# Filler matmuls in the waits of the layer ends, the last V tiles used in parts, and the last K transposed ahead of other VectorE work

## The chip, the cores and the metric

The kernel runs on one core of a Trainium2 chip. The metric is the time of one execution on the device, in microseconds (us). A profile's span runs from the first to the last instruction; in the runs here the time is 1.8 to 2.8 us longer than the span, mostly 1.9. The engines are called PE (TensorE), DVE (VectorE), ACT (ScalarE), POOL (GpSimd) and SP (SyncE, which issues the transfers). Lines such as L492 are lines of the kernel that was profiled.

## The reference, cut to what matters

Two layers, each a decode step of attention over a long cache, then a gated MLP. Batch 4, one query position, 32 query heads on 8 groups of K and V, 4096 cached positions, head size 128, all in bfloat16. Both layers read the same caches and weights.

```python
def _A_ref(x, k_cache, v_cache, wq, wo):        # caches: 4 x 8 x 4096 x 128
    q = (x @ wq).reshape(B, Sq, 32, 128).transpose(0, 2, 1, 3)
    k = jnp.repeat(k_cache, 4, axis=1)
    v = jnp.repeat(v_cache, 4, axis=1)
    p = _softmax(jnp.einsum("bhqd,bhkd->bhqk", q, k) * (128 ** -0.5))
    o = jnp.einsum("bhqk,bhkd->bhqd", p, v)
    return o.transpose(0, 2, 1, 3).reshape(B, Sq, 32 * 128) @ wo

def _B_ref(x, w_gate, w_up, w_down):
    return (_sigmoid(x @ w_gate) * (x @ w_up)) @ w_down

x = x + _A_ref(_layernorm(x), A_k_cache, A_v_cache, A_wq, A_wo)
x = x + _B_ref(_layernorm(x), B_w_gate, B_w_up, B_w_down)
# ... and both once more (layer 1)
```

## The kernel before

The cached tensors of one group and one batch entry are one tile of 1 MB. Eleven such tiles fit in a ring, and SP loads them in order: four K tiles, four V tiles, group after group. K is transposed in place by DVE (2.2 to 2.3 us a tile). The kernel puts instructions into one queue per engine, in program order, with semaphores for the dependencies. Layer 1 goes through the groups backwards, so that group 7, which was last in layer 0, is used again from the ring without a load:

```python
def done_with(n, kind):
    for b in range(B):
        if n == G - 1:
            slots[n + 1, kind, b] = slots[n, kind, b]   # group 7 stays for layer 1
        else:
            free.append(slots[n, kind, b])
    pump()                                              # issue loads into free slots
```

The consequence is that at the end of layer 0 no load can be issued until the first scores of layer 1 are done and free K of group 7. The parts of a group that the change touches:

```python
def keys_of(n, ahead):
    scores(n)                    # 32 matmuls, 16 x 512 each, four column groups
    done_with(n, "k")
    softmax(n)                   # DVE max, ACT exp
    tk(n + 1, ahead[:1])         # transposes of the next group's K on DVE
    probs_t(n)
    weights(n)                   # a chain of small DVE and ACT work
    tk(n + 1, ahead[1:])

def values(n):                   # 32 matmuls, four column groups (one for each batch entry)
    ...
def merge(n):
    # o_sb = O_ps * weights (ACT), then four transposes by PE with `ident`
    ...
def merge_sum(n):                # DVE tensor_reduce -> oT, bfloat16
    ...

for l in range(NLAYER):
    for n in range(l * G, (l + 1) * G - 2):
        keys_of(n, (0, 1, 2)); q_proj(n + 1); values_of(n, (3,))
    n = (l + 1) * G - 2
    keys_of(n, (0, 1, 2, 3))
    q_proj(n + 1)
    keys_of(n + 1, ())
    values_of(n)
    values_of(n + 1)
    residual(1.0, [])
    glu(l == NLAYER - 1)         # layer norm, gate/up, tanh, down
    if l < NLAYER - 1:
        layer_norm_q(); q_proj(n + 2)
```

The layer norm does mean, centring and transposition by PE and DVE, and then a variance matmul, a DVE step and a power on POOL for the reciprocal deviation (`rstd`).

## Time and profile before

| | before |
|---|---|
| time, median of 4 runs | 391.89 us (391.74 to 393.64) |
| the profiled run | 393.91 us, span 392.0 |
| read from HBM | 139.7 MB |
| no tile lands between | 216.0 and 236.0 us |
| last tile landed | 372.9 us, 19.0 us before the end of the span |

The landings are taken from the record of landings in the trace (the last of the 16 parts of each transfer). Outside the two gaps one tile lands every 2.5 us (K) or 2.7 us (V), or later where weights land between two tiles (8.5 us at most) or where one tile is late by itself (4.1 us at most).

The first view is the page of the kernel before: the granted PE clock in tenths in 40 slices of 9.8 us, and the busy tenths of the DMA engines.

```profile
PEclk9985565565655556585656565666666666655585
DMA  7999999999999999999999029999999999999900
```

The DMA row is at 9 nearly everywhere: the stream of tiles bounds the kernel. It has two holes, in slices 23 and 24 and at the end. PE is busy 43% of the span, so what PE or DVE do inside the stream costs little, and it is the two holes that can be shortened. (The clock records of this trace begin at 23.5 us; the 9s at the left of the clock row say nothing.)

The second view is the timeline of the first hole (start, duration, engine, line, operation, out<-in, how many; in brackets the idle time before and what ended it).

```profile
208.45 3.25 PE L492 MATMUL O_ps<-ring,pt_sb 128*16 128x512 bf16 x32 [6.29 <-DMA ring<-in_A_v_cache_dram]
...
212.58 0.66 PE L509 MATMUL M_ps<-ident,o_sb 128*128 128x128 f32 x4 [0.88 <-ACT o_sb L504]
...
216.35 1.67 PE L557 MATMUL PT_ps<-wg,xT 128*4 128x448 bf16 x16
...
217.80 1.71 PE L557 MATMUL O_ps<-wu,xT 128*4 128x448 bf16 x16
...
221.02 1.45 PE L593 MATMUL Y_ps<-wd,hT 128*4 128x128 bf16 x48 [0.32 <-DVE hT L587]
...
227.40 3.59 PE L416 MATMUL S_ps<-ring,qbd 128*16 128x512 bf16 x32 [0.98 <-ACT qbd L397]
```

This is one chain from the landing of the last V tile (208.4 us) to the end of the first scores (231.0 us): values (L492), merge (L509), gate and up (L557), down (L593), scores (L416). Now the same kernel by stretches: busy time of each engine with its count of instructions, the granted clock, DMA share, GB/s.

```profile
core 0: us, PE busy (x) PEld busy (x) DVE busy (x) ACT busy (x) POOL busy (x), PEclk, DMA share, GB/s
208.40:216.30 7.90, 5.34 (x57) 2.46 (x57) 1.06 (x6) 1.18 (x3) 0.00 (x0) 0.72 0.76 314
216.30:223.10 6.80, 5.27 (x94) 2.62 (x94) 1.35 (x5) 0.63 (x1) 0.55 (x1) 0.50 0.01 2
223.10:231.10 8.00, 5.66 (x57) 2.65 (x57) 0.75 (x5) 1.54 (x7) 0.55 (x1) 0.50 0.00 0
```

For two thirds of the chain the granted clock is 0.5, and the DMA engines move next to nothing. The timeline of the second hole:

```profile
355.54 6.66 DVE L407 STREAM_TRANSPOSE ring<-ring 128x2048 int32<-128x2048 int32 x3
...
362.34 3.59 PE L416 MATMUL S_ps<-ring,qbd 128*16 128x512 bf16 x32 [7.41 <-DVE ring L407]
...
370.75 3.59 PE L492 MATMUL O_ps<-ring,pt_sb 128*16 128x512 bf16 x32
...
376.41 1.90 PE L492 MATMUL O_ps<-ring,pt_sb 128*16 128x512 bf16 x32
...
382.95 1.67 PE L557 MATMUL PT_ps<-wg,xT 128*4 128x448 bf16 x16
...
384.40 1.71 PE L557 MATMUL O_ps<-wu,xT 128*4 128x448 bf16 x16
```

The last scores wait for three transposes. Of the two sets of values, which are 32 equal matmuls each, the first takes 3.59 us and the second 1.90: the same work, at half and at full clock (the clock records show 0.50 and 1.00 there).

### The profile page before, as it was taken

To read this page: it belongs to the slowest core of one execution; us is meant where nothing else is said; L and a number is where in the kernel's file an instruction comes from. 1 tells how busy PE (TensorE), PEld (TensorE's weight loads), DVE (VectorE), ACT (ScalarE), POOL (GpSimd) and SP (SyncE) were. 2 spreads that over 40 slices of the span, in tenths; PEclk is the share of its full clock that TensorE was granted. 3 is DMA by queue.
4 is the path that set the end of the run, shared out by engine and by line. 5 is a ranking of instruction groups with operands and counts; after the bars stand their busy time and mean duration, and the time that the engine had idled before them with its cause. 6 is when DMAs were issued, how large, how long until landed. Compare 5 with 4: busy or idle time off the path is not lost.

```text
span 392.0 us, 4800 instructions
## 1 busy us (share of the span) xinstructions
PE 168.5 (43%) x1998; PEld 71.5 (18%) x1998; DVE 191.6 (49%) x272; ACT 86.3 (22%) x171; POOL 9.4 (2%) x34
## 2 busy tenths in 40 slices
PE   0140722615435173341454746462634444441565
PEld 0120210202112121111112413221211111111123
DVE  3813715538175371768311138474829192858211
ACT  1130031031310313113210132313131313222310
POOL 6100000000000000000000000000000000000000
PEclk9985565565655556585656565666666666655585
DMA  7999999999999999999999029999999999999900
GB/s 307 403 385 407 393 380 417 387 413 397 384 412 385 410 390 405 421 414 343 395 388 366 2 97 381 418 390 416 394 411 397 407 403 400 423 407 387 352 2 2
DMA packets 48549, 140.04 MB, mean 357 GB/s; under 512 B 2192, under 2 KB 6544, under 8 KB 40848
## 3 DMA queue, kind: packets, MB, share of 16 engines
q1 hardware_dynamic: 48480, 139.73, 92.5%
q8 instruction: 16, 0.26, 0.3%
q14 instruction: 5, 0.04, 0.0%
q10 hardware_dynamic: 48, 0.01, 0.0%
HBM read 139.73 MB, written 0.00 MB: 356 GB/s over the span
## 4 chain that ended last, share of the span: by engine, by line
DMA 39%; PE 25%; DVE 18%; SPq 8%; ACT 7%; issue 2%; ACTq 0%; DVEq 0%
DMA ring<-in_A_k_cache_dram 36%; PE O_ps L492 13%; DVE ring L407 12%; PE S_ps L416 6%; SPq L248 5%; ACT p_sb L433 4%; SPq L270 3%; DMA ring<-in_A_v_cache_dram 2%; DVE ml L426 2%; ACT ee L468 1%; PE M_ps L509 1%; PE PT_ps L445 1%; ACT o_sb L504 1%; PE Y_ps L593 1%; PE Q_ps L391 1%
## 5 line engine op out<-in xcount | busy, mean ns | idle before, releaser
L407 DVE STREAM_TRANSPOSE ring<-ring 128x2048 int32<-128x2048 int32 x60 | 135.7, 2285 | 68.0 <-DMA ring<-in_A_k_cache_dram 68.0
L416 PE MATMUL S_ps<-ring,qbd 128*16 128x512 bf16 x512 | 56.6, 617 | 44.6 <-DVE ring L407 43.6
L433 ACT ACTIVATE p_sb<-S_ps,nbias,rs_q 128x1024 bf16<-128x1024 f32 x16 | 41.8, 2614 | 144.3 <-DVE nbias L429 144.3
L492 PE MATMUL O_ps<-ring,pt_sb 128*16 128x512 bf16 x512 | 55.3, 609 | 6.3 <-DMA ring<-in_A_v_cache_dram 6.3
L426 DVE TENSOR_REDUCE ml<-S_ps 128x1 f32<-128x1024 f32 x16 | 19.6, 1225 | 60.3 <-PE S_ps L416 60.3
L445 PE MATMUL PT_ps<-sel_p,p_sb 128*128 128x64 bf16 x128 | 9.7, 241 | 68.5 <-ACT p_sb L433 68.5
L391 PE MATMUL Q_ps<-qT,perm 128*128 128x16 bf16 x64 | 4.4, 179 | 66.5 <-ACT qT L388 66.5
L416 PEld LDWEIGHTS S_ps<-ring,qbd 128*16 128x16 bf16 x512 | 15.5, 120 | 75.0 <-issue 50.4
L504 ACT ACTIVATE o_sb<-O_ps,wcol 128x512 f32<-128x512 f32 x16 | 11.0, 688 | 53.4 <-PE O_ps L492 53.4
L445 PEld LDWEIGHTS PT_ps<-sel_p,p_sb 128*128 128x128 bf16 x128 | 7.2, 126 | 82.4 <-ACT p_sb L433 82.4
L492 PEld LDWEIGHTS O_ps<-ring,pt_sb 128*16 128x16 bf16 x512 | 16.3, 122 | 32.5 <-issue 24.8
L509 PE MATMUL M_ps<-ident,o_sb 128*128 128x128 f32 x64 | 13.7, 351 | 13.8 <-ACT o_sb L504 13.8
L468 ACT ACTIVATE ee<-dd,rs_q 128x16 f32<-128x16 f32 x16 | 4.9, 304 | 57.1 <-DVE dd L467 57.1
L520 DVE TENSOR_REDUCE oT<-M_ps 128x16 bf16<-128x64 f32 x16 | 3.6, 227 | 25.3 <-PE M_ps L509 25.2
L391 PEld LDWEIGHTS Q_ps<-qT,perm 128*128 128x128 bf16 x64 | 3.0, 107 | 67.8 <-ACT qT L388 67.8
L397 ACT ACTIVATE qbd<-Q_ps 32x64 bf16<-32x64 f32 x64 | 13.8, 215 | 6.4 <-PE Q_ps L391 5.9
L509 PEld LDWEIGHTS M_ps<-ident,o_sb 128*128 128x128 f32 x64 | 8.8, 174 | 27.7 <-ACT o_sb L504 27.7
L450 ACT ACTIVATE pt_sb<-PT_ps 128x512 bf16<-128x512 f32 x16 | 9.6, 597 | 11.2 <-PE PT_ps L445 11.2
L530 PE MATMUL Y_ps<-wo,oT 128*4 128x128 bf16 x256 | 7.7, 254 | 5.1 <-DVE oT L520 5.1
L366 POOL TENSOR_TENSOR rs_h<-vpe,mhalf 128x1 f32<-128x1 f32 x2 | 1.1, 552 | 361.8 <-DVE vpe L362 204.8
L383 PE MATMUL Q_ps<-xT,wq 128*128 128x4 bf16 x256 | 9.4, 168 | 0.0
L383 PEld LDWEIGHTS Q_ps<-xT,wq 128*128 128x128 bf16 x256 | 9.2, 109 | 0.0
(75 smaller groups left out, 87.0 us busy)
## 6 DMA issues: line engine op xcount, KB each, us to landing
ring<-in_A_k_cache_dram SPq DMA_DIRECT2D x60, 1024.0 KB, 13.9
ring<-in_A_v_cache_dram SPq DMA_DIRECT2D x60, 1024.0 KB, 16.0
wq<-in_A_wq_dram SPq DMA_DIRECT2D x4, 1024.0 KB, 14.0
wo<-in_A_wo_dram SPq DMA_DIRECT2D x4, 1024.0 KB, 14.0
wg<-in_B_w_gate_dram SPq DMA_DIRECT2D x1, 1792.0 KB, 15.1
wu<-in_B_w_up_dram SPq DMA_DIRECT2D x1, 1792.0 KB, 17.1
wd<-in_B_w_down_dram SPq DMA_DIRECT2D x1, 1536.0 KB, 14.2
wd_r<-in_B_w_down_dram SPq DMA_DIRECT2D x2, 128.0 KB, 14.3
```

The source lines that it names most:

```text
L248: S.put("sp", lambda e: e.dma_start(o, i), writes=[f"r{s}"], dma=f"r{s}")
L270: S.put("sp", lambda e: e.dma_start(o, i), writes=[key], dma=key)
L383: fns.append(lambda e, h=h, k=k, c0=c0: e.matmul(Q_ps[:, h * B:(h + 1) * B], lhsT=wq[:, k, c0:c0 + DH], rhs=xT[:, k, :], start=(k == 0), s ...
L397: fns.append(lambda e, a=a: e.activation(qbd[32 * a:32 * a + 32, qi, :, :, a * R:(a + 1) * R], Q_ps[32 * a:32 * a + 32, 64:128].rearrange( ...
L407: S.put("dve", lambda e: e.transpose(v, v), reads=[f"r{s}"], writes=[f"r{s}"])
L416: fns.append(lambda e, q=q, nn=nn, b=b, kt=kt: e.matmul(S_ps[32 * b:32 * b + 16, q * 512:(q + 1) * 512], lhsT=qbd[:, qi, b, nn, :], rhs=kt ...
L426: "dve", lambda e: e.tensor_reduce(ml[:, 0:1], S_ps[:], AX.X, ALU.max, negate=True),
L433: lambda e: e.activation(p_sb[:].rearrange("p tb (j q) -> p q tb j", q=4), S_ps[:].rearrange("p (q tb j) -> p q tb j", q=4, tb=8), ACTF.Ex ...
L445: fns.append(lambda e, tb=tb: e.matmul(PT_ps[:, tb * 64:(tb + 1) * 64], lhsT=p_sb[:, tb, :], rhs=sel_p[:], start=True, stop=True,))
L492: fns.append(lambda e, tb=tb, b=b, v=v: e.matmul(O_ps[32 * b:32 * b + 16, :], lhsT=pt[:, tb, 16 * b:16 * b + 16], rhs=v[:, :, tb, :], star ...
L504: "act", lambda e: e.activation(o_sb[:], O_ps[:], ACTF.Copy, scale=wc[:, 0:1]),
L509: fns.append(lambda e, a=a: e.transpose(M_ps[:, a * P:(a + 1) * P], o_sb[:, a * P:(a + 1) * P], ident[:]))
```

## The change

The intent: keep the PE clock up in the layer ends by constant matmuls whose result nobody reads ("fillers"); use the last V tiles as they land; and have most of the last K transposed before other DVE work. With it come a merge by matmuls instead of transposes, a later variance matmul, and a spread of q over two engines. The core of the diff:

```diff
+    def warm(us):
+        fn = lambda e: e.matmul(
+            S_ps[:, 0:256], lhsT=perm[:, 0, :], rhs=perm[:, 0:2, :].rearrange("p n x -> p (n x)"), start=True, stop=True
+        )
+        S.put("pe", [fn] * round(us / 0.107), reads=["perm"], writes=["S"])
...              # warm(0.1) to warm(0.6) after steps of the layer norm, q, gate/up, down, merge
-    def layer_norm(sel, sel_key, mult, rs, rs_key):     # variance matmul inside
+    def layer_norm():
+    def rstd(sel, sel_key, mult, rs, rs_key):           # variance matmul, vpe, POOL power
...
+            if w is wg:                                 # in glu
+                S.put("pe", fns[:4], reads=["xT", key], writes=[bkey])
+                rstd(mean_s, "mean_s", 4.0, rs_h, "rs_h")
+                fns = fns[4:]
...
+        if first:                                       # in q_proj, first of a layer
+            rstd(mean_b, "mean_b", float(DH), rs_q, "rs_q")
+        spread("act", (0, 1) if first else (0, 1, 2, 3))
+        if first:
+            spread("dve", (2, 3))
...
-            fns.append(lambda e, a=a: e.transpose(M_ps[:, a * P:(a + 1) * P], o_sb[:, a * P:(a + 1) * P], ident[:]))
+            fns.append(lambda e, a=a: e.matmul(
+                M_ps[:, 0:16], lhsT=o_sb[:, a * P:(a + 1) * P], rhs=sel_o[:, a, :], start=(a == 0), stop=(a == 3),
+            ))
...
+    def last_values_of(n):
+        if n < G:
+            warm(1.0)
+            values(n, (0,))
+            warm(1.0)
+            values(n, (1, 2))
+        else:
+            values(n, (0, 1, 2))
+        values(n, (3,))
+        ...
...
-            keys_of(n, (0, 1, 2))
+            if G <= n < G + 4:
+                keys_of(n, mid=(0,), late=(1, 2))
+            else:
+                keys_of(n, late=(0, 1, 2))
...
-        keys_of(n, (0, 1, 2, 3))
+        keys_of(n, early=(0, 1), mid=(2,), late=(3,))
```

In `keys_of`, `early` stands on DVE before the softmax's maximum, `mid` where the first transpose stood, `late` after the weights.

## The prediction

> **What bounds the kernel.** Mostly the reading of the caches. The slices show the DMA engines at 9 tenths in all but the first slice, slices 23 and 24 and the last two, at about 400 GB/s. By the landings recorded in the trace, one 1 MB tile lands every 2.5 to 2.7 us, except (a) one tile 1.4 us late at 49 us, (b) nothing between 216.0 and 236.0 us, (c) nothing after 372.9 us. (b) and (c) are the two layer ends: chains of small work with no transfer beside them, because layer 1 reuses resident tiles and asks for the next when its first scores are done. Only these can pay.
>
> The chain of the first layer end (timeline): last V tile lands 208.4, values 208.45 to 211.7, merge, output projection, layer norm, gate/up 216.35 to 219.5, down 221.0 to 222.7, layer norm, query, first scores 227.4 to 231.0. The windows table gives a granted clock of 0.58 there. The same 32 matmuls took 3.59 us at clock 0.5 and 1.90 us at 1.0 (values at 376.4). The Trainium skill, "TensorE: Matmul & The Clock Gate", Part 1, says the clock halves after an idle window of about 3.4 us and rises after a busy one; this trace agrees: the clock records change in steps of 3.413 us, and windows busy 79% or more were followed by full clock, up to 76% not.
>
> **What the change does** (us saved, from trace durations)
>
> First layer end:
> - V burst: only 8 matmuls left after the last tile, about 1.7 at full clock instead of 3.25: +1.6.
> - Merge by f32 matmuls (two passes each, as the mean matmul has) instead of transposes: 0.66 becomes about 1.1: -0.4.
> - Variance matmul behind the first gate matmuls: +0.75; second layer norm +0.6.
> - Gate/up at full clock, then bounded by the rstd chain through GpSimd: +1.6 warm, -0.3 cold; expected +1.3.
> - Down, small matmuls: +0.5. Spread of q over two engines, 0.90 to 0.45: +0.45.
> - First scores warm: +1.7 at even odds (the second layer norm leaves PE about 70% busy): +0.85.
> Sum +5.6.
>
> Second layer end: the last scores start at 362.3, behind three transposes of 2.2 us that follow the softmax weights; K15 lands from 343.9 to 351.4, so only one has to stay behind: 4.5 earlier. The values follow, but two bursts cost about 1.7 more PE time, since V15 has landed by then. Values end about 2 earlier. Then merge -0.4, layer norm +0.75, gate/up +1.5, down +0.3. Sum +4.
>
> Streamed part: first K transpose no longer ahead of the weights: the late tile at 49 us, +1.4.
>
> Sum 11 us, discounted for windows that stay cold and for fillers that then take twice as long: 382 us, range 378.5 to 387. Faster by over 2% 0.72, within 2% 0.27, slower 0.01.
>
> **What would show it.** The gap without landings 14 to 15 us instead of 20; granted clock near 1.0 from the last values to down; gate/up together 1.6 to 2 us; last scores about 4.5 us closer to the last landing; tail after the last landing about 15 us instead of 19; the tile at 49 us on time; tile spacing unchanged.
>
> **What would make it wrong.** Fillers that leave the windows below the threshold: the chain keeps its cold lengths and pays the fillers too (near 386 to 388). Merge matmuls dearer than estimated. Second-layer bursts running cold (2 x 3.4 us).

## The result, and the profile after

| | before | after |
|---|---|---|
| time, median of 4 | 391.89 us (391.74 to 393.64) | 385.84 us (385.36 to 386.12) |
| profiled run: time, span | 393.91, 392.0 | 385.65, 383.8 |
| gap without landings | 216.0 to 236.0: 20.0 us | 216.1 to 232.7: 16.6 us |
| last landing | 372.9 | 369.8 |
| from there to the end of the span | 19.0 us | 14.0 us |

The ratio is 0.9834, 95% interval 0.9804 to 0.9864. Ratios are the mean time of one kernel's fast runs over that of the other's of the same rounds, so not quite the ratio of the medians quoted. The gain of 1.7% lies within 2%, to which the prediction gave 0.27 (0.72 to a larger gain); the predicted range held, and the predicted 382 was 3.8 us too low.

The page of the kernel after, slices again:

```profile
PEclk9995565555555555556678986765655566665689
DMA  7999999999999999999999319999999999999940
```

The clock row stands at 6 to 9 in slices 20 to 26, around the hole in the middle, where it was 5 and 6, and at 8 and 9 in the last two slices, where it was 8 and 5. The timeline of the first layer end:

```profile
200.57 1.89 PE L511 MATMUL O_ps<-ring,pt_sb 128*16 128x512 bf16 x8
...
206.09 5.41 PE L511 MATMUL O_ps<-ring,pt_sb 128*16 128x512 bf16 x24 [2.54 <-DMA ring<-in_A_v_cache_dram]
...
212.35 1.06 PE L528 MATMUL M_ps<-sel_o,o_sb 128*128 128x16 f32 x8
...
216.38 0.74 PE L574 MATMUL PT_ps<-wg,xT 128*4 128x448 bf16 x12
...
216.95 0.93 PE L574 MATMUL O_ps<-wu,xT 128*4 128x448 bf16 x16
...
219.42 0.84 PE L616 MATMUL Y_ps<-wd,hT 128*4 128x128 bf16 x48
...
224.28 3.53 PE L435 MATMUL S_ps<-ring,qbd 128*16 128x512 bf16 x32 [0.84 <-DVE qbd L416]
```

Gate and up (L574) and down (L616) now run at full clock. But the 24 matmuls of the last two bursts took 5.41 us after a wait of 2.54 us, and the first scores (L435) still take 3.53 us. The stretches of this kernel, each one clock window of 3.41 us:

```profile
203.74:207.15 3.41, 1.06 (x10) 0.52 (x12) 0.00 (x0) 0.00 (x0) 0.00 (x0) 1.00 1.07 398
207.15:210.56 3.41, 3.39 (x13) 0.97 (x10) 0.00 (x0) 0.00 (x0) 0.00 (x0) 0.50 1.04 426
210.56:213.97 3.41, 3.04 (x35) 1.86 (x32) 0.17 (x1) 0.69 (x1) 0.00 (x0) 1.00 0.98 406
...
220.80:224.22 3.42, 2.10 (x30) 1.34 (x29) 1.14 (x6) 1.11 (x5) 0.44 (x1) 1.00 0.02 5
```

The first of these windows is 31% busy and the next runs at 0.5; the last one shown is 61% busy, and the scores that follow it are the slow ones. This is one trace. The changed kernel was traced once more in experiment 5, and there the values of the first layer end ran at full clock. The timeline of the second layer end:

```profile
352.20 2.27 DVE L426 STREAM_TRANSPOSE ring<-ring 128x2048 int32<-128x2048 int32 x1
...
354.61 3.25 PE L435 MATMUL S_ps<-ring,qbd 128*16 128x512 bf16 x32 [3.02 <-DVE ring L426]
...
368.85 2.89 PE L511 MATMUL O_ps<-ring,pt_sb 128*16 128x512 bf16 x32
...
376.63 0.74 PE L574 MATMUL PT_ps<-wg,xT 128*4 128x448 bf16 x12
...
377.19 0.93 PE L574 MATMUL O_ps<-wu,xT 128*4 128x448 bf16 x16
```

Only one transpose (352.20) stands between the weights and the last scores. The chain from step to step, from the two timelines (the landing of the first line is that of the last V tile):

| step | before | after | saved |
|---|---|---|---|
| first end: last landing to end of values | 3.3 | 2.8 | 0.5 |
| end of values to residual | 2.3 | 2.6 | -0.3 |
| xT ready to product of gate and up (L568, L590) | 4.0 | 2.3 | 1.7 |
| hT ready to residual (down) | 1.8 | 1.1 | 0.7 |
| residual to first scores | 4.7 | 3.9 | 0.8 |
| first scores | 3.6 | 3.5 | 0.1 |
| second end: last landing to end of values | 5.4 | 1.9 | 3.5 |
| end of values to last residual | 11.0 | 9.0 | 2.0 |

### The profile page after: what moved, and what is told of

It reads as the page before. It is cut to its first block, busy times and chain, and to the rows that moved or that the text cites. A ratio compares the mean times of both kernels' runs of the same rounds, so it can differ in the third digit from the quotient of the medians.

```text
span 383.8 us, 5091 instructions
## 1 busy us (share of the span) xinstructions
PE 187.3 (49%) x2143; PEld 88.6 (23%) x2143; DVE 194.2 (51%) x276; ACT 84.5 (22%) x167; POOL 9.9 (3%) x37
## 5 line engine op out<-in xcount | busy, mean ns | idle before, releaser
L426 DVE STREAM_TRANSPOSE ring<-ring 128x2048 int32<-128x2048 int32 x60 | 137.2, 2299 | 39.0 <-DMA ring<-in_A_k_cache_dram 38.5
L435 PE MATMUL S_ps<-ring,qbd 128*16 128x512 bf16 x512 | 56.4, 616 | 38.6 <-DVE ring L426 37.8
L511 PE MATMUL O_ps<-ring,pt_sb 128*16 128x512 bf16 x512 | 59.8, 597 | 4.5 <-DMA ring<-in_A_v_cache_dram 4.4
L435 PEld LDWEIGHTS S_ps<-ring,qbd 128*16 128x16 bf16 x512 | 15.8, 121 | 69.0 <-issue 43.1
L528 PE MATMUL M_ps<-sel_o,o_sb 128*128 128x16 f32 x128 | 22.1, 308 | 10.8 <-ACT o_sb L522 10.5
L511 PEld LDWEIGHTS O_ps<-ring,pt_sb 128*16 128x16 bf16 x512 | 18.2, 120 | 33.7 <-issue 29.4
L528 PEld LDWEIGHTS M_ps<-sel_o,o_sb 128*128 128x128 f32 x128 | 20.6, 245 | 22.1 <-ACT o_sb L522 22.0
L474 DVE STREAM_TRANSPOSE tr<-ml 128x64 f32<-128x64 f32 x16 | 3.8, 237 | 28.8 <-ACT p_sb L452 28.8
L537 DVE CAST oT<-M_ps 128x16 bf16<-128x16 f32 x16 | 2.5, 155 | 30.3 <-PE M_ps L528 30.3
L547 PEld LDWEIGHTS Y_ps<-wo,oT 128*4 128x4 bf16 x256 | 4.1, 93 | 45.2 <-DVE oT L537 45.2
L414 ACT ACTIVATE qbd<-Q_ps 32x64 bf16<-32x64 f32 x60 | 12.8, 214 | 6.4 <-PE Q_ps L401 5.9
L335 PE MATMUL S_ps<-perm 128*128 128x256 bf16 x81 | 14.0, 288 | 0.0
```

The costliest lines, as they stand in the source:

```text
L335: fn = lambda e: e.matmul(S_ps[:, 0:256], lhsT=perm[:, 0, :], rhs=perm[:, 0:2, :].rearrange("p n x -> p (n x)"), start=True, stop=True)
L414: fns.append(lambda e, o=o, i=i: e.activation(o, i, ACTF.Copy))
L426: S.put("dve", lambda e: e.transpose(v, v), reads=[f"r{s}"], writes=[f"r{s}"])
L435: fns.append(lambda e, q=q, nn=nn, b=b, kt=kt: e.matmul(S_ps[32 * b:32 * b + 16, q * 512:(q + 1) * 512], lhsT=qbd[:, qi, b, nn, :], rhs=kt ...
L511: fns.append(lambda e, tb=tb, b=b, v=v: e.matmul(O_ps[32 * b:32 * b + 16, :], lhsT=pt[:, tb, 16 * b:16 * b + 16], rhs=v[:, :, tb, :], star ...
L528: fns.append(lambda e, a=a: e.matmul(M_ps[:, 0:16], lhsT=o_sb[:, a * P:(a + 1) * P], rhs=sel_o[:, a, :], start=(a == 0), stop=(a == 3),))
```

## The experiments

**Theories.** The main theory (T): the clock is what the fillers buy, and it is granted window by window; the part of the first layer end that did not shorten (values and scores) is PE work that fell into half-clock windows, because the window before had PE waiting. The new order of K pays in the second layer end. Rivals: (R1) the fillers buy nothing and the reordered chain is all; (R2) the order of K is worth nothing, since the stream bounds; (R3) the bursts save what was predicted; (R4) the wait for the third V tile and the slow scores are out of reach of fillers. Each batch of experiments ran on a chip of its own, beside 11 runs of the kernel before. The first batch did not hold the changed kernel itself: its comparisons with the changed kernel go through the ratios to before.

### 1. No fillers

```diff
     def warm(us):
         ...
-        S.put("pe", [fn] * round(us / 0.107), reads=["perm"], writes=["S"])
+        return
```

> The changed kernel without any filler matmul. Theory (the fillers buy full clock at both layer ends): gate/up and down run cold again, about 1.0 us for gate/up and 0.6 us for down at each end, so 388.5 to 389.5 us, and the granted clock between the first layer's last values and the next scores falls from about 0.9 to about 0.6. Rival (the fillers buy nothing, all the gain is the reordering): 385.5 to 386.2 us, even a little faster.

Measured: 393.44 us (389.65 to 394.32), ratio 0.9984, interval 0.9933 to 1.0036. The whole gain is gone, more than T expected. In the trace the gap is 17.6 us, but the tail after the last landing is 19.4 us instead of 14.0. In the timeline of the second layer end:

```profile
370.22 5.13 PE L511 MATMUL O_ps<-ring,pt_sb 128*16 128x512 bf16 x32
...
380.75 1.29 PE L574 MATMUL PT_ps<-wg,xT 128*4 128x448 bf16 x12
...
381.83 1.71 PE L574 MATMUL O_ps<-wu,xT 128*4 128x448 bf16 x16
```

The last values take 5.13 us: three column groups' matmuls, then the fourth's, nearly all at half clock. So the bursts are a loss where the clock is down. At the first end of the same trace it was not down: without any filler, the windows from 204.4 to 214.6 us had full clock, and the last burst ended 1.9 us after its tile. R1 falls.

### 2. No bursts

```diff
-            warm(1.0)
-            values(n, (0,))
-            warm(1.0)
-            values(n, (1, 2))
-        else:
-            values(n, (0, 1, 2))
-        values(n, (3,))
+            warm(2.0)
+        values(n, range(B))
```

> The changed kernel with the last V tiles used in one go of 32 matmuls at both ends, the same number of fillers before it. Theory (the bursts gained nothing, because PE waited 2.5 us for the third tile and the following matmuls ran cold): 385.5 to 386.4 us. Rival (bursts save about 1.6 us at the first end, as predicted): about 387.4 us.

Measured: 388.18 us (387.21 to 389.3), ratio 0.9872, interval 0.9829 to 0.9914. My expectation fell: the bursts are not worthless. In the timeline:

```profile
208.87 3.59 PE L511 MATMUL O_ps<-ring,pt_sb 128*16 128x512 bf16 x32 [7.54 <-DMA ring<-in_A_v_cache_dram]
...
218.84 1.53 PE L574 MATMUL O_ps<-wu,xT 128*4 128x448 bf16 x16
```

All fillers went at once, then PE waited 7.54 us. The values ran at half clock and the clock was down again for gate and up. The gap without landings is 18.9 us against 16.6 with bursts; the tail is 14.0 us in both. So in this pair of traces the bursts of the first end are worth 2.3 us, less by what they shorten themselves (0.8 us: values end 3.6 instead of 2.8 us after the landing) than by the clock after them: gate and up took 3.6 us together instead of 2.1. That the bursts did this by keeping PE at work is the reading of T; another trace of the changed kernel (experiment 5) has a gap of 15.5 us, so the worth of the bursts depends on the trace. In the second end they made no difference.

### 3. The old order of K transposes

```diff
-            if G <= n < G + 4:
-                keys_of(n, mid=(0,), late=(1, 2))
-            else:
-                keys_of(n, late=(0, 1, 2))
+            keys_of(n, mid=(0,), late=(1, 2))
...
-        keys_of(n, early=(0, 1), mid=(2,), late=(3,))
+        keys_of(n, mid=(0,), late=(1, 2, 3))
```

> The changed kernel with the K transposes in the order of before. Theory (the order brings the last values about 3.5 us closer to the last landing): 389.0 to 389.8 us. Rival (the stream of tiles bounds and the order is worth nothing): 385.6 to 386.2 us.

Measured: 391.13 us (388.55 to 392.26), ratio 0.9937, interval 0.9891 to 0.9983. In its trace the last scores start 10.6 us before the last landing, where the changed kernel starts them 15.2 us before it, and the values end 6.5 us after it instead of 1.9. The order is worth 4.6 us of position, and 4.5 was predicted. The time lies above the range expected; against the changed kernel's ratio of 0.9834 the intervals don't overlap. R2 falls.

### 4. The new order alone, on the kernel before

```diff
-            keys_of(n, (0, 1, 2))
+            if G <= n < G + 4: keys_of(n, mid=(0,), late=(1, 2))
+            else: keys_of(n, late=(0, 1, 2))
-        keys_of(n, (0, 1, 2, 3))
+        keys_of(n, early=(0, 1), mid=(2,), late=(3,))
```

> The kernel before with only the new order of K transposes. Theory: about 3 us of the 3.5 us shows here too, 388.3 to 389.2 us. Rival: 391.7 to 392.2 us.

Measured: 392.12 us (389.36 to 393.54), ratio 0.995, interval 0.9895 to 1.0005. That is less than the 3 us expected: 0.5 us by medians and 2.2 by means, with an interval that includes no gain. The scores are as early as in the changed kernel (15.1 us before the last landing), but:

```profile
372.02 3.59 PE L492 MATMUL O_ps<-ring,pt_sb 128*16 128x512 bf16 x32 [0.79 <-issue]
...
382.58 1.71 PE L557 MATMUL O_ps<-wu,xT 128*4 128x448 bf16 x16
```

PE reached the last values ahead of the last tile, waited, and then ran them, gate/up and down at half clock, where the first trace of before had the values at full clock (1.90 us). In this trace what the order gains is mostly handed back through the clock: the values end 3.7 us after the last landing instead of 5.4, and the tail is 18.2 us instead of 19.0.

### 5. The changed kernel once more

No edit.

> The changed kernel once more, on the chip of this batch, as the yardstick for the others: 385.4 to 386.2 us as before, if the chip matters little; the earlier batch had kernels about 2 us apart on another chip.

Measured: 385.74 us (384.38 to 386.88); the kernel before had a median of 396.1 us (392.0 to 397.34) in the same rounds. Ratio 0.9771, interval 0.9719 to 0.9823. The changed kernel's time is the same as on the first chip. The kernel before now had 4 runs from 392.0 to 393.7 and 7 from 395.8 to 397.3. So the size of the gain, 1.7% or 2.3%, depends mostly on which of these the kernel before falls into (see 11 and 12).

The trace of this run differs from the first trace of the same kernel. Its values of the first layer end, and one of its clock windows:

```profile
206.14 1.90 PE L511 MATMUL O_ps<-ring,pt_sb 128*16 128x512 bf16 x16 [2.03 <-DMA ring<-in_A_v_cache_dram]
208.74 1.89 PE L511 MATMUL O_ps<-ring,pt_sb 128*16 128x512 bf16 x8 [0.70 <-DMA ring<-in_A_v_cache_dram]
```

```profile
202.36:205.77 3.41, 1.75 (x13) 0.89 (x10) 0.00 (x0) 0.00 (x0) 0.00 (x0) 1.00 1.05 387
```

PE waited 2.03 us for the third tile, much as in the first trace. But the clock windows begin at other places of the chain: this one is 51% busy, the next 69%, and after both the clock stayed full. In the first trace the window from 203.74 us was 31% busy and the next ran at 0.5. So the last burst ended 1.9 us after its tile instead of 2.8, and the gap without landings was 15.5 us instead of 16.6. The first scores were slow again (3.30 us).

### 6. The empty waits filled

```diff
-            warm(1.0)
-            values(n, (0,))
-            warm(1.0)
-            values(n, (1, 2))
+            warm(1.0)
+            for b in range(3):
+                values(n, (b,))
+                warm(0.8)
...      # layer norm: warm(0.2), warm(0.1) -> warm(0.3), warm(0.2); first q: warm(0.1) -> warm(0.2)
             rstd(mean_b, "mean_b", float(DH), rs_q, "rs_q")
+            warm(0.7)
```

> The changed kernel with the waits filled that its trace leaves empty: each last V tile of the first layer end used as it lands with eight fillers between, and more fillers in the layer norm and in the 0.84 us before the first scores of layer 1. Theory[...]: first scores 1.9 us, gap without landings 14.5 to 15 us, time 1.5 to 2.5 us under the changed kernel of this batch. Rival (clock windows are out of reach, or the fillers only delay): within 0.5 us of it, first scores still 3.5 us.

Measured: 384.75 us (384.36 to 386.4), ratio 0.975, interval 0.9702 to 0.9798. That is 1.0 us under experiment 5 by medians and 0.6 by means, with ranges that overlap: less than T expected. Its trace (of a run of 386.07 us) has the first scores at full clock, and the last burst ends 1.9 us after its tile, as it did in experiment 5 without these fillers:

```profile
208.92 1.89 PE L512 MATMUL O_ps<-ring,pt_sb 128*16 128x512 bf16 x8
...
217.28 1.32 PE L575 MATMUL O_ps<-wu,xT 128*4 128x448 bf16 x16
...
224.95 2.04 PE L436 MATMUL S_ps<-ring,qbd 128*16 128x512 bf16 x32
```

R4 falls for the scores, in this one trace; for the values nothing is shown. But gate and up have become slow: a half-clock window came in just there, at 214.7 us, although the window before it had PE busy. So the gap without landings, 15.6 us, is no shorter than in experiment 5. This pointed to the merge.

### 7. The fillers alone, on the kernel before

The edit adds the fillers of the change at the same places of the kernel before (layer norm, first q, gate/up, down, merge, last values), and nothing else.

> The kernel before with the fillers alone: no bursts, no new order, merge, variance or spread as before. Theory (fillers buy gate/up and down at full clock at both ends, about 2 us each): 387.5 to 389.5 us, 3 to 4 us under the kernel before. Rival (fillers pay only with the reordered chain): over 390.5 us.

Measured: 389.1 us (387.2 to 392.17), ratio 0.9855, interval 0.9798 to 0.9913. As T expected. On the same chip the whole change has 0.9771, so the fillers alone are about 60% of it, 5.8 us of 9.4 by the means.

### 8. The old variance matmul and the old spread of q

```diff
-    def layer_norm():
+    def layer_norm(*r):
         ...
         warm(0.1)
+        rstd(*r)
...      # rstd taken out of glu and q_proj again
-        spread("act", (0, 1) if first else (0, 1, 2, 3))
-        if first:
-            spread("dve", (2, 3))
+        spread("act", (0, 1, 2, 3))
```

> The changed kernel with the variance matmul in its old place and q spread by ScalarE alone. Theory: 0.75 us for each of two gate/up starts, 0.6 and 0.45 us at the second layer norm, less what the rstd chain through GpSimd hides: 1.5 to 2.5 us over the changed kernel of this batch. Rival (off the chain): within 0.5 us of it.

Measured: 388.59 us (387.67 to 388.9), ratio 0.9833, interval 0.9786 to 0.9879. That is 2.85 us over experiment 5 on the same chip: these two small edits are worth somewhat more than expected. In its trace gate and up of the first layer end took 2.75 us, partly at half clock, against 2.10 in experiment 5, so a part of this may be the clock.

### 9. The old merge

The four transposes, `ident` and the sum on DVE are put back in the changed kernel, in place of the merge by f32 matmuls; the fillers stay.

> The changed kernel with the merge by transposes and a sum on VectorE, as before. Theory (the f32 merge matmuls cost 1.06 us against 0.66, at each end one of them lies on the chain, and the cast is 0.06 us shorter than the sum): 0.5 to 0.9 us faster than the changed kernel, 385.0 us. Rival (the merge matmuls are the better form, or they are hidden): same or slower than 385.8 us.

Measured: 382.86 us (381.69 to 384.19), ratio 0.9728, interval 0.9688 to 0.9768. Faster than the changed kernel by 2.9 us by medians (on another chip; the ratios to before are 0.9728 and 0.9771, with intervals that overlap; but all six runs lie below all ten of the changed kernel). The direct difference is what was predicted: 0.66 us for the transposes against 1.06. The rest came with the clock. In its trace the full clock lasts from 197.5 to 228.2 us without a break (199.0 to 222.8 in experiment 5), the gap is 13.9 us (15.5 there), and the last burst of the values and the first scores, with no more fillers than the changed kernel has, are:

```profile
208.37 1.89 PE L509 MATMUL O_ps<-ring,pt_sb 128*16 128x512 bf16 x8 [0.71 <-DMA ring<-in_A_v_cache_dram]
...
222.70 2.02 PE L433 MATMUL S_ps<-ring,qbd 128*16 128x512 bf16 x32 [0.84 <-DVE qbd L414]
```

### 10. The filled waits, and the merge in bfloat16

```diff
-    sel_o = sb("sel_o", [P, 4, 16])
+    sel_o = sb("sel_o", [P, 4, 16], bf)
+    o_bf = sb("o_bf", [P, D], bf)
...
-            "act", lambda e: e.activation(o_sb[:], O_ps[:], ACTF.Copy, scale=wc[:, 0:1]),
+            "act", lambda e: e.activation(o_bf[:], O_ps[:], ACTF.Copy, scale=wc[:, 0:1]),
...
-                M_ps[:, 0:16], lhsT=o_sb[:, a * P:(a + 1) * P], rhs=sel_o[:, a, :], ...
+                M_ps[:, 0:16], lhsT=o_bf[:, a * P:(a + 1) * P], rhs=sel_o[:, a, :], ...
```

> The kernel with the filled waits (run e6_warm_gap), and the merge matmuls in bfloat16: one pass instead of two and a quick weight load. Theory: 0.26 to 0.4 us instead of 1.07 at each end, so 1.3 to 1.6 us under e6_warm_gap, 383.2 us, and nearer to 383 in every run, since a window with 1.07 us of weight loading in it went cold there. Rival (the merge is hidden): 384.8 us.

Measured: 381.48 us (381.3 to 381.81), correct, ratio 0.9691, interval 0.9653 to 0.973. This is the fastest version, and its six runs lie within 0.5 us, where experiment 6 had 2.0 and the kernel before 5.4. Against experiment 6, on another chip, it gains 3.3 us by medians, more than the 0.8 us per end that the merge itself became shorter (0.26 us for four matmuls against 1.07 for eight passes). Here are two clock windows of each trace at the same place of the chain, first of experiment 6, then of this one:

```profile
211.26:214.68 3.42, 2.87 (x35) 1.80 (x34) 0.83 (x5) 0.36 (x1) 0.00 (x0) 1.00 0.94 388
214.68:218.10 3.42, 3.42 (x33) 1.44 (x37) 0.33 (x2) 1.00 (x3) 0.55 (x1) 0.51 0.10 43
```

```profile
210.85:214.27 3.42, 2.83 (x39) 1.35 (x36) 1.01 (x6) 1.02 (x3) 0.00 (x0) 1.00 0.96 400
214.27:217.68 3.41, 3.31 (x47) 1.76 (x43) 1.00 (x3) 0.63 (x1) 0.55 (x1) 1.00 0.20 82
```

PE is busy 2.87 of 3.42 us in the one (84%) and 2.83 in the other (83%). After the first the clock falls to 0.51, after the second it stays at 1.00. The window of experiment 6 holds eight f32 merge passes, 1.07 us of busy time. One guess is that these count for little in what the clock goes by. It is not shown: the window of the changed kernel from 210.56 us, printed above, holds eight such passes too (89% busy) and was followed by full clock, and a window of the same trace from 80.86 us with no f32 work in it, at half clock and 84% busy, was followed by half clock. What experiments 9 and 10 show is that the chain is faster without the f32 merge.

### 11 and 12. The kernel before, traced twice more

No edit.

> The kernel before, unchanged, for one more trace: its times fall in two groups, near 392 and near 396.5 us. Theory (where the free-running clock windows fall decides it): in a run of the slow group the last values of layer 1 or one of the gate/up bursts runs at half clock where the first trace had full clock, and tile spacing is the same. Rival (the DMA is slower in such runs): landings are spread wider than 2.5 to 2.7 us.

> The same once more, to have a fair chance of one trace of the slow group: 392 or 396.5 us, with the same two theories.

Measured: 396.92 us (span 394.9) and 392.79 us (span 390.5), one of each group. Landings are spaced alike, 2.5 to 2.7 us. The gap without landings is 21.3 and 20.2 us, the tail 20.6 and 17.7 us. The second layer end of the slow one, then of the fast one:

```profile
385.83 1.67 PE L557 MATMUL PT_ps<-wg,xT 128*4 128x448 bf16 x16
...
387.28 1.71 PE L557 MATMUL O_ps<-wu,xT 128*4 128x448 bf16 x16
```

```profile
383.70 0.93 PE L557 MATMUL PT_ps<-wg,xT 128*4 128x448 bf16 x16
...
384.46 0.93 PE L557 MATMUL O_ps<-wu,xT 128*4 128x448 bf16 x16
```

The same matmuls, at half and at full clock. In the slow run no window from 202.8 to 250.5 us has full clock; in the fast one those from 211.2 and from 231.7 us have, and all from 378.5 to 388.7 us, of which the slow run has only 3.4 us. So in this pair of traces the two groups of times of the kernel before are a matter of where the clock windows fall on its chain. The idea of slower transfers falls.

## Why the prediction was right or wrong

**The bound and the place of the gain: right.** The stream kept its pace (layer 1 from first to last landing: 136.9 us before, 137.1 after), and both holes shortened.

**"V burst: +1.6": failed in the first trace of the changed kernel, came close in the second.** It gave 0.5 us in the first and 1.35 in the second (experiment 5). The step assumed full clock at the last tile. In both traces PE had over 2 us without work before the third tile, because fillers of a fixed number ended early; in the first the next clock window ran at half clock, in the second the windows fell differently and it did not. The kernel is the same in both, so which of the two values a trace shows is luck. With full clock the 8 matmuls take 1.89 us (experiments 5, 6 and 9), close to the 1.7 assumed. But so do all 32 in four column groups (1.90). The Trainium skill, "TensorE: Matmul & The Clock Gate", Part 3, says that matmuls in different column groups run at the same time; these numbers agree. So one burst after the last tile beats the whole set only when the whole set would be cold.

**"First scores warm: +0.85" at even odds: did not come.** They took 3.3 to 3.6 us, mostly at half clock, in both traces of the changed kernel and in experiments 1, 2, 3 and 8. Seven more fillers in the 0.84 us before them, with the other added ones, brought 2.04 us (experiment 6), and the old merge brought 2.02 us without any (experiment 9).

**"Merge -0.4": right for itself, wrong in effect.** Itself 1.06 us against 0.66. In the whole it cost several times that: undoing it gave 2.9 us by medians, for both ends, of which the matmuls themselves are 0.8. Between the traces of experiments 5 and 9, the first scores alone account for 1.3 us, mostly at half clock in the one and at full clock in the other. This is the largest mis-sized term, and the prediction named it only as a chance. Why the clock does better without this merge stays open (experiment 10).

**"Variance +0.75" and "gate/up +1.3" (+1.5 in the second end): counted twice.** From xT ready to the product of gate and up the trace says 4.0 us before and 2.3 after, together 1.7 (second end 1.6), not 2.05 and 2.25. The bound by the rstd chain, which the prediction gave itself, already held the earlier start.

**Down, second layer norm, spread: nearly right.** 0.7 and 0.8 us, predicted 0.5 and 1.05. Experiment 8 gives 2.85 us for variance and spread at both ends; the terms predicted were 0.75 twice, 0.6 and 0.45, that is 2.55.

**"Second layer end +4": right, a little low.** Scores 4.6 us closer to the last landing, as said. The last values ended 3.5 us closer, not 2, and the rest gave 2.0. The tail is 5.0 us shorter.

**"The late tile at 49 us: +1.4": failed.** That tile came on time, but another, at 38.7 us, came 1.2 us late, and layer 0's last landing stayed at 216.1. A late tile between 36 and 50 us is in every trace, and the windows table of before shows the DMA share at 1.03 or more from 42 to 50 us, so it was no starvation. In each of the fourteen traces the late tile lands 2.2 to 4.4 us after the first 16 KB fetch of instructions in the stream began (46.7 us before, 35.3 after); but many later fetches delay no tile, and in experiment 1 a tile at 240.4 us came 4.1 us after the one before it. That the fetch is the cause was not tested.

**The base.** The prediction took 11 us off 392, which is the span of the profiled run as well as the median time. That run took 393.91 us. Its trace lost 8.2 us of span (392.0 to 383.8), the medians 6.0 us.

**The clock threshold: failed.** The prediction gave a busy share above which a window is followed by full clock (cut from its text above, because the trace before doesn't show it). In that trace, windows busy 80% (from 235.1 us) and 87% (from 381.9 us) were followed by half clock and one of 78% (from 146.4 us) by full clock; in experiment 5, at full clock, a window of 51% was followed by full clock. No single share of PE's busy time sorts these windows. What is right is the step of 3.413 us and the two values, 0.5 and 1.0; on these the Trainium skill, "TensorE: Matmul & The Clock Gate", Part 1, agrees with all traces.

Together: the mechanisms were right except for the threshold, and the prediction put too much on the first layer end (5.6 us for what became 3.4 in the first trace and, against the same trace before, 4.4 in the second), because it priced the fillers as if they kept nearly every window warm.

## What to carry to other kernels

When a chain of small matmuls decides the time, price each step at the clock it will get, and look at the windows before it: a gain in waiting (an earlier arrival, a split) can be handed back as half-speed work. Try filling every wait up to the arrival that ends it, and try replacing small f32 matmuls in such a chain: here that paid 2.9 and 3.3 us by medians, though why is not shown. And take several runs and traces of both kernels: where the clock windows fall differs from run to run, one trace can mistake luck for the change, and a part of the change's worth is that it spreads less (2.5 us against 5.3 over the runs of experiment 5's chip).

## What the Trainium skill lacked or had wrong

- "TensorE: Matmul & The Clock Gate", Part 1, does not say how busy a window must be, or which work counts. Two windows at full clock with PE busy 84% and 83% were followed by clock 0.51 and 1.00 (experiments 6 and 10), one of 51% by 1.00 (experiment 5) and one of 53% by 0.50 (before, from 211.2 us).
- The same part says that the ramp's penalty, that of the first warm-up, is under 1% of a typical kernel's span. It has no figure for how much a kernel whose clock changes throughout differs from run to run. Here the kernel before took 392.79 and 396.92 us (1.05% apart) in two traces that differ in the clock windows, and fillers alone gave a ratio of 0.9855.
- The same page, Part 3, has a measured speed-up for three column tiles, and none for four. Here 32 matmuls in four column groups took 1.90 us and 8 in one group 1.89 us at full clock: a factor of 4.
- The same page, Part 4, says that full clock does not engage for transposes. Here four of them took 1.12 us at a granted clock of 0.5 and 0.66 us at 1.0 (both in the trace before), and a chain with them kept full clock for 30.7 us (experiment 9). Whether they count as work for the clock no run shows by itself.
